# Pooled attention into a four-expert layer: the first tile's loads and order, the first keys' pooling, and the slots of later key and value loads

## The chip, the core and the metric

The kernel runs on one core of a Trainium2 chip. The core has TensorE (matrix products, written to PSUM), VectorE, ScalarE, GpSimd and SyncE, each with its own instruction stream, and 16 DMA engines that all of them share. SyncE and ScalarE issue plain transfers and transposing transfers through the hardware queue; GpSimd issues transfers through the software queue, which can convert f32 to bf16 on the way. The metric is the device time of one execution in microseconds. The profile adds one execution recorded by the hardware profiler.

## The reference

Eight batches, eight heads, 576 tokens of 64 values. Keys and values are averaged over groups of 8 tokens, so each head has 72 pooled keys and values. The attention output, all heads of a token side by side (512 values), feeds four experts, each two matrix products with a ReLU between; the experts' outputs are added with weights from `domain_probs`.

```python
k_p = k.reshape(B, H, Sp, pool, D).mean(axis=3)          # Sp = 72, pool = 8, D = 64
v_p = v.reshape(B, H, Sp, pool, D).mean(axis=3)
scores = scale * np.matmul(q, k_p.transpose(0, 1, 3, 2))
scores = scores - np.max(scores, axis=-1, keepdims=True)
attn = np.exp(scores)
attn = attn / (np.sum(attn, axis=-1, keepdims=True) + 1e-09)
x = np.matmul(attn, v_p)            # (8, 8, 576, 64), then to (4608, 512)
p = domain_probs / (domain_probs.sum(-1, keepdims=True) + 1e-09)
for e in range(4):                  # w1: 512 x 1024, w2: 1024 x 512
    h = np.maximum(x @ w1[e], 0.0)
    out += p[:, e:e + 1] * (h @ w2[e])
```

## The kernel before

**Tiles and groups.** The 4608 tokens are 36 tiles of 128 (`t`); four tiles make a group of 512 (`g`). Attention is computed tile by tile, the expert layer group by group: `up` (L447) makes one block of 128 hidden columns for all 512 tokens of a group (four products of 128x512), `down` (L479) makes the output of one tile from the eight hidden blocks (eight products of 128x512). `collect` (L491) adds a tile's output, weighted, on VectorE and after the fourth expert stores it through SyncE.

**Attention of a tile.** `turn_q` (L301) puts head pairs of the queries on the partitions (for tiles 0 to 8 by TensorE transposes and a ScalarE copy, for later ones by a transposing DMA on SyncE). `scores` (L316) multiplies them with the pooled keys `kT`; its PSUM tile `sc` has a single buffer. `maxima` and `less` (together `less_max`) work on VectorE, `expo` on ScalarE. `attn_T` (L387) turns the exponentials, `context` or `context_rows` (L404) multiplies them with the pooled values `vbd`, a block-diagonal spread made with `mask_v`. In rows form (tile 0 and tiles from 8 on) the division by the row sums is done after the product with the values (`x_sb`, L416); otherwise `normalise` (L377) comes before the turn. For tiles from 8 on `attnT` and `xT` are made by transposing DMAs too.

**Pooling.** `prep_k` (L245) adds the eight rows of a group in three folds on VectorE and places each sum twice, masked, into `kpad`; `prep_kT` (L256) turns it into `kT`, for batches from 2 on by a transposing DMA on SyncE (L259). `prep_v` makes `vbd` likewise. Batch 0 is special: `fold_keys0` folds its keys in three parts as they land, `turn_keys0` transposes them on TensorE, `take_keys0` copies the right halves into the zeroed `kT[0]`; its values are summed by eight products with an identity matrix (`sum_values0`, L611) and spread on VectorE (`spread_values0`, L620).

**Order.** Every engine runs its instructions in the order of the Python code (`manual_schedule`). GpSimd's queue begins with the keys and values of batch 0, then the weights of expert 0 and what follows (L145 to L175). The start (L650 to L716) is written out by hand: tile 0 to tile 3 of group 0 are attended, and expert 0's first products are done tile by tile (`up_tile`, L460). `idle_products(n)` (L568) multiplies a zero tile with itself n times. `split_q(c)` (L564) is ScalarE's conversion of tile c's queries out of `qg`, which one SyncE transfer fills for the four tiles of group 0, token `4p + c` on partition p.

After the start a loop of 36 steps with 12 slots each issues `up` of the next step and `down` of this one, and after each slot what `plan` holds for it. `plan_tile(t, slot)` places a tile's attention, `gate(t)` (a GpSimd copy that waits for the tile's `x_sb`) and `load_q(t + 3)` behind it; `plan_batch(b, slot)` places `prep_k`, `prep_kT` and `prep_v` of a batch at slot + 5, + 8 and + 9, one step before the first tile that needs the batch. The loads of keys and values for batches from 3 on stand in the list `waiting`; for each tile from 8 on, in order, one of them is taken off the list and placed at `base + 6` (L559 to L561), where `base - 2` is the slot in which the tile's plan begins, and so directly behind that tile's gate and query load. `done_batches` counts the batches whose preparation has been planned.

Of the kernel before, what the change touches and what calls it, by code (L numbers as in the profile page):

```python
# [10 lines left out]
ALU = mybir.AluOpType  # L11
AX = mybir.AxisListType
BF16 = mybir.dt.bfloat16
F32 = mybir.dt.float32
# [3 lines left out]
def kernel(  # L18
# [102 lines left out]
    def load_w2(e):  # L121
# [5 lines left out]


    qg = raw.tile([P, H, TPG, D], F32, name="qg")
    nc.sync.dma_start(  # L130
        out=qg[:], in_=q[0][:, 0:G, :].rearrange("h (p c) d -> p h c d", c=TPG)
    )
    dp0 = const.tile([P, TPG, E], F32, name="dp0")
    nc.sync.dma_start(
        out=dp0[:], in_=moe_domain_probs[0:G].rearrange("(p c) e -> p c e", c=TPG)
# [48 lines left out]
    def make_mask_v():  # L184
        nc.vector.tensor_copy(
            out=mask_v[:].rearrange("p a z y d -> p (a z y) d"),
            in_=own[:].rearrange("p a z y -> p (a z y)").unsqueeze(2).to_broadcast(
                [P, NPAIR * 4, D]
            ),
        )  # L190
# [141 lines left out]
    def maxima(t):  # L332
        mxs[t] = soft.tile([P, 2, 4], F32, name="mx")
        nc.vector.reduce_max(out=mxs[t][:], in_=by_head(t), axis=AX.X)  # L334
# [213 lines left out]
    for g in range(2, NG):  # L548
        for i in range(TPG):
            t = g * TPG + i  # L550
            base = (E * g - 5 + i) * SLOTS
            last_b = ((t + 1) * P - 1) // S
            if last_b >= done_batches:
                plan_batch(last_b, base - 2 - SLOTS)
                done_batches += 1
                if last_b + 2 < B:
                    waiting += [(load_k, last_b + 2), (load_v, last_b + 2)]
            plan_tile(t, base - 2, -9 if t > 2 * TPG else 0)
            if waiting:  # L559
                load, b = waiting.pop(0)  # L560
                at(base + 6, load, b)  # L561


    def split_q(c):  # L564
        nc.scalar.copy(out=qrow[c][:], in_=qg[:, :, c, :])


    def idle_products(n):  # L568
        ps = ps_o.tile([P, DM], F32, name="o_ps")
        for _ in range(n):  # L570
            nc.tensor.matmul(ps[:], lhsT=still[:, 0:P], rhs=still[:], start=True, stop=True)  # L571
# [2 lines left out]

    kT[0] = prep.tile([P, NB, P], BF16, name="kT")
    nc.vector.memset(kT[0][:], 0.0)
    kpad0 = prep.tile([P, NB, 2, D], BF16, name="kpad")
    kT_ps = ps_h.tile([P, NB, P], BF16, tag="h", name="kT_ps")

    def fold_keys0(p1, i0, i1):  # L580
        rows = kraw[0][0:p1, i0:i1]
        for n in (4, 2):
            w = n * D
            nc.vector.tensor_add(
                out=rows[:, :, 0:w], in0=rows[:, :, 0:w], in1=rows[:, :, w:2 * w]
            )
        twice = [p1, i1 - i0, 2, D]
        nc.vector.tensor_tensor(
            out=kpad0[0:p1, i0:i1], in0=rows[:, :, 0:D].unsqueeze(2).to_broadcast(twice),
            in1=rows[:, :, D:2 * D].unsqueeze(2).to_broadcast(twice), op=ALU.add,  # L590
        )

    def turn_keys0(p1, i0, i1):
        for i in range(i0, i1):
            nc.tensor.transpose(
                kT_ps[:, i, 0:p1], kpad0[0:p1, i].rearrange("p z d -> p (z d)"),
                ident[0:p1, 0:p1],
            )

    def take_keys0():  # L600
        for z in range(2):
            dst, src = (
                x[z * D:(z + 1) * D].rearrange("x i p -> x (i p)")[:, 0:ROWS].rearrange(
                    "x (a y j) -> x a y j", y=2, j=SP
                )[:, :, z]
                for x in (kT[0], kT_ps)
            )
            nc.vector.tensor_copy(out=dst, in_=src)

# [38 lines left out]
        nc.scalar.copy(out=xT[0][:, :, 0:P], in_=ps[:])  # L648

    idle_products(14)  # L650
    split_q(0)
    split_q(1)
    turn_q(0)
    turn_q(1)
    for part in ((P, 0, 2), (P, 2, 4), (TAIL, 4, 5)):
        fold_keys0(*part)
        turn_keys0(*part)
        idle_products(2)
    take_keys0()
    make_mask_v()  # L660
    scores(0)
    split_q(2)
    turn_q(2)
    less_max(0)
    split_q(3)
    expo(0)
    idle_products(2)
    spread_values0(sum_values0())
    attn_T(0)
    scores(1)  # L670
    maxima(1)
    idle_products(2)
    sums0()
    turn_q(3)
    idle_products(1)
    xT[0] = grp.tile([P, KC, G], BF16, name="xT")
    x0 = context_rows(0)
    idle_products(4)
    turn_x0(x0)
    less(1)  # L680
    expo(1)
    idle_products(2)
    up_tile(0, 0)
    scores(2)
    normalise(1)
    idle_products(4)
    less_max(2)
    domain_probs0()
    for t in range(1, TPG):
        attn_T(t)  # L690
        if t + 1 < TPG:
            expo(t + 1)
        if t == 1:
            idle_products(3)
        else:
            down(0, t - 1, 0, FB // 2)
        context(t)
        if t == 1:
            scores(3)
            up_tile(0, t)  # L700
            down(0, t - 1)
        else:
            down(0, t - 1, FB // 2, FB)
            up_tile(0, t)
        if t + 1 < TPG:
            normalise(t + 1)
        if t == 1:
            less_max(3)
        if t == TPG - 1:
            make_mask_k()  # L710
        collect(0, t - 1)
# [49 lines left out]
```

## Time and profile before

| | us |
|---|---|
| median of 3 runs | 555.86 (554.24 to 556.35) |
| the profiled execution | 556.4 |
| its span, first to last instruction | 554.4 |
| first product of the expert loop (L453) | 36.82 |
| first product of `up_tile` (L469) | 19.01 |
| first key part folded (L584) | 7.79 |
| all of `kT[0]` copied (L608) | 11.76 |
| last 40 products of the chain of waits (L486) begin | 542.05 |

The span is the time between the first and the last instruction of the profiled execution; some 2 us lie around it. A row of the timeline gives start, length, engine, line, operation, and in brackets how long the engine had been idle and what ended that. L numbers are lines of the kernel before. "Landing" of a DMA counts from its issue to the end of its last write. The page's 40 slices show the DMA engines and the granted TensorE clock (in tenths of full speed) over the span:

```profile
PEclk9999999899999999999999999999999999999999
DMA  9999918455745534366535553334333431111002
```

The DMA engines are full for about the first 70 us (the first five slices of 13.9 us), while weights, keys, values and queries arrive; after that they are busy about half the time or less.

### The profile page before, as it was taken

How to read it: one execution, taken by the hardware profiler on the slowest of the kernel's cores; microseconds unless marked ns; L12 is line 12 of the kernel's file. 1: busy time of each engine (PE TensorE's matmuls, PEld its weight loads, DVE VectorE, ACT ScalarE, POOL GpSimd, SP SyncE). 2: the span in 40 equal slices, each digit the busy share in tenths (PEclk: the TensorE clock that was granted, in tenths of full speed). 3: DMA queues.
4: the chain of work that ended last, by engine and by line, in shares of the span. 5: the costliest groups of instructions: out<-in, count | busy, mean ns of one | idle time of the engine just before them, and what ended most of it. 6: DMA issues, size and time to landing. Idle time of an engine off the chain costs nothing.

```text
span 554.4 us, 7323 instructions
## 1 busy us (share of the span) xinstructions
PE 542.0 (98%) x2929; PEld 261.3 (47%) x2929; DVE 264.7 (48%) x456; ACT 213.5 (39%) x355; POOL 70.6 (13%) x120
## 2 busy tenths in 40 slices
PE   7899998999999999999999999999999999999997
PEld 3664553444444444444444444444444444444443
DVE  4874846344644445644463444744474444422223
ACT  3554653233333333333333333333333333333330
POOL 7234002111101100112011100101010000000000
PEclk9999999899999999999999999999999999999999
DMA  9999918455745534366535553334333431111002
GB/s 200 206 200 200 199 8 137 74 80 79 122 82 83 84 59 99 53 84 74 116 48 77 84 116 41 52 41 98 60 54 40 74 74 32 21 39 38 1 0 77
DMA packets 110689, 45.84 MB, mean 83 GB/s; under 512 B 87584, under 2 KB 106016, under 8 KB 110656
## 3 DMA queue, kind: packets, MB, share of 16 engines
q0 software_dynamic: 51472, 22.03, 32.3%
q1 hardware_dynamic: 59184, 23.35, 17.8%
q8 instruction: 23, 0.38, 0.3%
q14 instruction: 10, 0.08, 0.0%
HBM read 45.16 MB, written 9.44 MB: 98 GB/s over the span
## 4 chain that ended last, share of the span: by engine, by line
PE 93%; DMA 3%; DVE 2%; ACT 1%; issue 0%; POOL 0%; SPq 0%; POOLq 0%
PE o_ps L486 44%; PE h_ps L453 43%; PE x_ps L410 2%; PE sc L320 2%; DMA kT<-kpad 1%; PE h_ps L469 1%; DMA kraw<-in_k_dram 1%; PE x_ps L436 1%; PE o_ps L571 0%; DVE acc L501 0%; PE at_ps L394 0%; ACT attnT L395 0%; PE qT_ps L310 0%; DVE kraw L235 0%; DVE vraw L235 0%
## 5 line engine op out<-in xcount | busy, mean ns | idle before, releaser
L457 ACT ACTIVATE h_sb<-h_ps 128x512 bf16<-128x512 f32 x280 | 167.2, 597 | 301.3 <-PE h_ps L453 301.1
L453 PE MATMUL h_ps<-xT,w 128*128 128x512 bf16 x1120 | 275.2, 380 | 0.0
L486 PE MATMUL o_ps<-w,h_sb 128*128 128x512 bf16 x1152 | 272.3, 379 | 0.0
L486 PEld LDWEIGHTS <-h_sb 128*128 128x128 bf16 x1152 | 112.5, 98 | 134.5 <-issue 1.1
L501 DVE SCALAR_TENSOR_TENSOR acc<-o_ps,p_sb,acc 128x512 f32<-128x512 f32 x108 | 81.0, 750 | 180.4 <-PE o_ps L486 180.4
L453 PEld LDWEIGHTS <-w 128*128 128x128 bf16 x1120 | 106.1, 98 | 117.2 <-issue 0.6
L497 DVE TENSOR_SCALAR acc<-o_ps,p_sb 128x512 f32<-128x512 f32 x36 | 27.0, 750 | 62.1 <-PE o_ps L486 62.1
L525 POOL COPY gated<-x_sb 1x1 bf16<-1x1 bf16 x28 | 7.8, 278 | 372.2 <-DVE x_sb L416 372.2
L334 DVE TENSOR_REDUCE mx<-sc 128x8 f32<-128x576 f32 x36 | 27.2, 756 | 14.1 <-PE sc L320 14.1
L108 POOL DMA_DIRECT2D qrow<-in_q_dram x36 | 30.5, 850 | 26.3 <-DMA w<-in_moe_w_dram 15.2
L338 DVE TENSOR_TENSOR d_sb<-sc,mx 128x576 f32<-128x576 f32 x36 | 27.3, 757 | 1.2
L416 DVE SCALAR_TENSOR_TENSOR x_sb<-x_ps,rs 128x512 bf16<-128x512 f32 x29 | 20.1, 692 | 12.5 <-PE x_ps L410 12.1
L351 ACT ACTIVATE attn<-d_sb 128x576 bf16<-128x576 f32 x29 | 19.8, 682 | 3.6 <-DVE d_sb L338 0.5
L372 DVE TENSOR_REDUCE es<-attn 128x8 f32<-128x576 bf16 x28 | 20.8, 744 | 0.0
L320 PE MATMUL sc<-kT,qT 128*128 128x144 bf16 (+1 forms) x160 | 15.3, 229 | 3.1 <-DMA kT<-kpad 2.9
L320 PEld LDWEIGHTS <-qT 128*128 128x128 bf16 (+1 forms) x160 | 11.2, 101 | 11.5 <-issue 5.5
L410 PEld LDWEIGHTS <-attnT 128*128 128x128 bf16 (+1 forms) x160 | 12.2, 100 | 7.3 <-issue 1.3
L410 PE MATMUL x_ps<-vbd,attnT 128*128 128x192 bf16 (+5 forms) x160 | 14.7, 231 | 0.0
L571 PE MATMUL o_ps<-still 128*128 128x512 bf16 x38 | 11.8, 436 | 1.3 <-DVE still L144 1.3
L235 DVE TENSOR_TENSOR vraw<-vraw 128x1280 bf16<-128x1280 bf16 (+1 forms) x14 | 9.2, 654 | 0.2
L235 DVE TENSOR_TENSOR kraw<-kraw 128x1280 bf16<-128x1280 bf16 (+1 forms) x14 | 9.0, 640 | 0.2
L469 PE MATMUL h_ps<-xT,w 128*128 128x128 bf16 x128 | 7.8, 219 | 0.7 <-ACT xT L442 0.4
(76 smaller groups left out, 148.9 us busy)
## 6 DMA issues: line engine op xcount, KB each, us to landing
out_dram<-acc SPq DMA_DIRECT2D x36, 256.0 KB, 2.0
vraw<-in_v_dram POOLq DMA_DIRECT2D x8, 512.0 KB, 7.6
w<-in_moe_w_dram POOLq DMA_DIRECT2D x8, 512.0 KB, 16.1
w<-in_moe_w_dram POOLq DMA_DIRECT2D x4, 1024.0 KB, 16.2
kraw<-in_k_dram POOLq DMA_DIRECT2D x7, 512.0 KB, 7.3
qrow<-in_q_dram POOLq DMA_DIRECT2D x28, 128.0 KB, 3.8
qg<-in_q_dram SPq DMA_DIRECT2D x1, 1024.0 KB, 5.7
kraw<-in_k_dram POOLq DMA_DIRECT2D x2, 256.0 KB, 6.7
```

What stands on the lines that cost most here:

```text
L108: nc.gpsimd.dma_start(out=qrow[t][at:at + n], in_=q[b][:, tok:tok + n, :].rearrange("h p d -> p h d"),)
L320: nc.tensor.matmul(sc[at:at + n, pair // 2, (pair % 2) * PW:(pair % 2 + 1) * PW], lhsT=qT[t][:, pair, at:at + n], rhs=kT[b][:].rearrange(" ...
L334: nc.vector.reduce_max(out=mxs[t][:], in_=by_head(t), axis=AX.X)
L338: nc.vector.tensor_tensor(out=st[t][:], in0=by_head(t), in1=mxs[t][:].unsqueeze(3).to_broadcast([P, 2, 4, SP]), op=ALU.subtract,)
L372: nc.vector.reduce_sum(out=es[:], in_=e, axis=AX.X)
L410: nc.tensor.matmul(ps[at:at + n, h0 * D:(h0 + c1 - c0) * D], lhsT=attnT[t][:, i, at:at + n], rhs=flat[:, c0 * D:c1 * D], start=(i == 0), s ...
L416: nc.vector.scalar_tensor_tensor(out=x_sb[:].rearrange("p (h d) -> p h d", d=D), in0=ps[:].rearrange("p (h d) -> p h d", d=D), scalar=V_ME ...
L453: nc.tensor.matmul(ps[:], lhsT=w1_sb[e][:, kc, fb * P:(fb + 1) * P], rhs=xT[g][:, kc, :], start=(kc == 0), stop=(kc == KC - 1),)
L457: nc.scalar.activation(out=hs[s][:, fb, :], in_=ps[:], func=ACT.Relu)
L486: nc.tensor.matmul(ps[:], lhsT=hs[s][:, fb, i * P:(i + 1) * P], rhs=w2_sb[e][:, fb, :], start=(fb == 0), stop=(fb == FB - 1),)
L497: nc.vector.tensor_scalar_mul(out=accs[t][:], in0=ps[:], scalar1=p_sb[:, e, t:t + 1])
L501: nc.vector.scalar_tensor_tensor(out=accs[t][:], in0=ps[:], scalar=p_sb[:, e, t:t + 1], in1=accs[t][:], op0=ALU.mult, op1=ALU.add,)
```

## The change

Six things change. (1) The first SyncE transfer fetches only tile 0's queries; the other three tiles' queries are fetched by one transfer that ScalarE issues behind `split_q(0)`. (2) The keys of batch 0 are no longer folded on VectorE and transposed: 45 products with the identity add the eight rows and turn them at once into an f32 PSUM tile of the `sc` pool, the two halves of the partitions summing the same eight rows in another order. (3) `make_mask_v` comes first on VectorE. (4) `split_q`, `turn_q` of tiles 1 to 3 move behind `scores(0)`, `maxima(1)`, `context_rows(0)`, `expo(1)` and `scores(2)`; `context_rows(0)` follows `sums0` directly. (5) Fewer idle products stand at other places, 33 where there were 38, and `expo(2)` comes behind `context(1)`. (6) In the planner a waiting load is placed only at a tile t for which the batch of tile t + 1's last token is among those already planned.

```diff
@@ -127,9 +127,8 @@
 
 
     qg = raw.tile([P, H, TPG, D], F32, name="qg")
-    nc.sync.dma_start(
-        out=qg[:], in_=q[0][:, 0:G, :].rearrange("h (p c) d -> p h c d", c=TPG)
-    )
+    q0 = q[0][:, 0:G, :].rearrange("h (p c) d -> p h c d", c=TPG)
+    nc.sync.dma_start(out=qg[:, :, 0, :], in_=q0[:, :, 0, :])
     dp0 = const.tile([P, TPG, E], F32, name="dp0")
     nc.sync.dma_start(
         out=dp0[:], in_=moe_domain_probs[0:G].rearrange("(p c) e -> p c e", c=TPG)
@@ -556,7 +555,8 @@
                 if last_b + 2 < B:
                     waiting += [(load_k, last_b + 2), (load_v, last_b + 2)]
             plan_tile(t, base - 2, -9 if t > 2 * TPG else 0)
-            if waiting:
+
+            if waiting and ((t + 2) * P - 1) // S < done_batches:
                 load, b = waiting.pop(0)
                 at(base + 6, load, b)
 
@@ -574,36 +574,32 @@
 
     kT[0] = prep.tile([P, NB, P], BF16, name="kT")
     nc.vector.memset(kT[0][:], 0.0)
-    kpad0 = prep.tile([P, NB, 2, D], BF16, name="kpad")
-    kT_ps = ps_h.tile([P, NB, P], BF16, tag="h", name="kT_ps")
-
-    def fold_keys0(p1, i0, i1):
-        rows = kraw[0][0:p1, i0:i1]
-        for n in (4, 2):
-            w = n * D
-            nc.vector.tensor_add(
-                out=rows[:, :, 0:w], in0=rows[:, :, 0:w], in1=rows[:, :, w:2 * w]
-            )
-        twice = [p1, i1 - i0, 2, D]
-        nc.vector.tensor_tensor(
-            out=kpad0[0:p1, i0:i1], in0=rows[:, :, 0:D].unsqueeze(2).to_broadcast(twice),
-            in1=rows[:, :, D:2 * D].unsqueeze(2).to_broadcast(twice), op=ALU.add,
-        )
-
-    def turn_keys0(p1, i0, i1):
+    kT_ps = ps_s.tile([P, 2, 512], F32, name="sc")[:].rearrange("p g x -> p (g x)")
+
+
+
+    def sum_keys0(p1, i0, i1):
         for i in range(i0, i1):
-            nc.tensor.transpose(
-                kT_ps[:, i, 0:p1], kpad0[0:p1, i].rearrange("p z d -> p (z d)"),
-                ident[0:p1, 0:p1],
-            )
+            cols = slice(i * P, i * P + p1)
+
+            def add(half, r0, n, **flags):
+                nc.tensor.matmul(
+                    kT_ps[half, cols], lhsT=kraw[0][0:p1, i, r0 * D:(r0 + n) * D],
+                    rhs=ident[0:p1, 0:p1], skip_group_check=True, **flags,
+                )
+
+            for r in range(POOL - 1):
+                add(slice(0, P), r, 2, start=(r == 0 and i in (0, NB - 1)), stop=False)
+            add(slice(0, D), POOL - 1, 1, start=False, stop=True)
+            add(slice(D, P), 0, 1, start=False, stop=True)
 
     def take_keys0():
         for z in range(2):
             dst, src = (
-                x[z * D:(z + 1) * D].rearrange("x i p -> x (i p)")[:, 0:ROWS].rearrange(
-                    "x (a y j) -> x a y j", y=2, j=SP
-                )[:, :, z]
-                for x in (kT[0], kT_ps)
+                x[z * D:(z + 1) * D, 0:ROWS].rearrange("x (a y j) -> x a y j", y=2, j=SP)[
+                    :, :, z
+                ]
+                for x in (kT[0][:].rearrange("x i p -> x (i p)"), kT_ps)
             )
             nc.vector.tensor_copy(out=dst, in_=src)
 
@@ -648,55 +644,56 @@
         nc.scalar.copy(out=xT[0][:, :, 0:P], in_=ps[:])
 
     idle_products(14)
+    make_mask_v()
     split_q(0)
+    nc.scalar.dma_start(out=qg[:, :, 1:TPG, :], in_=q0[:, :, 1:TPG, :])
+    turn_q(0)
+    for part in ((P, 0, 2), (P, 2, 4), (TAIL, 4, 5)):
+        sum_keys0(*part)
+    take_keys0()
+    idle_products(3)
+    scores(0)
     split_q(1)
-    turn_q(0)
     turn_q(1)
-    for part in ((P, 0, 2), (P, 2, 4), (TAIL, 4, 5)):
-        fold_keys0(*part)
-        turn_keys0(*part)
-        idle_products(2)
-    take_keys0()
-    make_mask_v()
-    scores(0)
-    split_q(2)
-    turn_q(2)
     less_max(0)
-    split_q(3)
     expo(0)
     idle_products(2)
     spread_values0(sum_values0())
     attn_T(0)
     scores(1)
     maxima(1)
+    split_q(2)
     idle_products(2)
     sums0()
-    turn_q(3)
-    idle_products(1)
     xT[0] = grp.tile([P, KC, G], BF16, name="xT")
     x0 = context_rows(0)
-    idle_products(4)
+    turn_q(2)
+    idle_products(3)
     turn_x0(x0)
     less(1)
     expo(1)
+    split_q(3)
     idle_products(2)
     up_tile(0, 0)
     scores(2)
+    turn_q(3)
     normalise(1)
-    idle_products(4)
+    idle_products(2)
     less_max(2)
     domain_probs0()
     for t in range(1, TPG):
         attn_T(t)
-        if t + 1 < TPG:
-            expo(t + 1)
         if t == 1:
             idle_products(3)
-        else:
+        elif t + 1 < TPG:
+            expo(t + 1)
+        if t > 1:
             down(0, t - 1, 0, FB // 2)
         context(t)
         if t == 1:
+            expo(2)
             scores(3)
+            idle_products(2)
             up_tile(0, t)
             down(0, t - 1)
         else:
```

## The prediction

> **What bounds the kernel now.** I read the page's engine shares first, then TensorE's waits after the start, the stretches around the one wait found there, the chain of waits through it, and last the timeline and DMA queues of the start.
>
> ```profile
> PE 542.0 (98%) x2929; PEld 261.3 (47%) x2929; DVE 264.7 (48%) x456; ACT 213.5 (39%) x355; POOL 70.6 (13%) x120
> ```
>
> TensorE is busy 542.0 of 554.4 us, so only its 12.4 idle us, stretches at a low clock and the start (where "busy" includes 38 idle products) can be won. After the start (36.8 us) its waits have a single line:
>
> ```profile
> PE sc L320 <- DMA kT<-kpad: 2.9, 1, 2.9
> ```
>
> That is tile 9's scores waiting for the transposed keys of batch 2. The timeline's GpSimd rows, the chain, and the stretches around it (columns: stretch, length, busy us of PE, PEld, DVE, ACT, POOL, granted clock, DMA share, GB/s):
>
> ```profile
> 89.07 0.88 POOL L108 DMA_DIRECT2D qrow<-in_q_dram  x1
> 89.94 0.76 POOL L80 DMA_DIRECT2D kraw<-in_k_dram  x1
> ...
> 89.62 7.65 DMA kT<-kpad
> 97.27 0.14 issue
> 97.41 0.64 PE sc L320 x4
> 98.04 1.71 PE h_ps L453 x4
> 99.75 2.15 PE o_ps L486 x8
> ...
> 94.50:97.40 2.90, 0.03 (x1) 0.02 (x1) 0.00 (x0) 0.60 (x1) 0.00 (x0) 0.94 1.06 210
> 97.40:100.50 3.10, 3.09 (x11) 1.42 (x12) 1.51 (x2) 0.71 (x2) 0.00 (x0) 0.51 0.45 123
> ```
>
> The key transpose is issued at 89.62 and lands after 7.65 us; a key load (batch 3) goes out 0.32 us after it. After the wait TensorE runs for 3 us at clock 0.51.
>
> In the start, the timeline's rows that set the first expert product:
>
> ```profile
> 12.72 1.25 PE L614 MATMUL v_ps<-vraw,ident 128*128 128x320 bf16 x8
> 14.01 1.29 DVE L623 TENSOR_TENSOR vbd<-v_ps,mask_v 128x512 bf16<-128x512 f32 x2
> 15.59 0.76 DVE L334 TENSOR_REDUCE mx<-sc 128x8 f32<-128x576 f32 x1 [0.28 <-PE sc L320]
> 16.40 0.17 DVE L640 TENSOR_SCALAR es<-es_ps 128x8 f32<-128x8 f32 x1
> 17.19 0.69 DVE L416 SCALAR_TENSOR_TENSOR x_sb<-x_ps,rs 128x512 bf16<-128x512 f32 x1 [0.39 <-PE x_ps L410]
> 19.01 1.95 PE L469 MATMUL h_ps<-xT,w 128*128 128x128 bf16 x32 [0.24 <-ACT xT L648]
> ```
>
> The chain of waits names the keys (issued 1.32, second part landed 9.05, kT done 11.77). But the values bind almost as soon: they are issued at 3.39 and 4.15 and take 8.8 and 8.2 us, so they land at 12.19 and 12.35, and v_ps, vbd, the second maxima and x_sb follow each other from there. This decides what the start can win.
>
> **Part 1: key loads moved away from key transposes (L559).** By the new condition load_k(3) leaves slot 42 (the slot of prep_kT(2)) for slot 54. The queue shifts by one place: key and value loads of batches 3 to 5 go into slots 54, 66, 78, 102, 114, 126; those of batches 6 and 7 stay. Only slot 126 is new, and it has no key transpose.
>
> What it removes: scores(9) could have started at 93.50 + 0.86 = 94.36 (the four products before it, at the chain's price for four) and started at 97.41: 3.05 us. Then 0.64 + 1.71 + 2.15 = 4.50 us of products stand where the chain at 80 us has 0.25 + 0.86 + 1.73 = 2.84: 1.66 us of low clock. Together 4.7 us.
>
> Is the wait gone then? The other five key transposes have no key load beside them, but the same query load just before and stores behind; they land after 4.3, 4.1, 3.7, 4.0 and 4.5 us, and none is waited for. Here 94.36 - 89.62 = 4.74 us are free. So 0 us of wait is left, at worst 7.65 - 4.74 = 2.9 again if the key load was not the cause. I take 4.7.
>
> What moves: each load issues two DMAs on GpSimd's queue behind gate(t) and load_q; the next in that queue is the gate a tile (14 us) later, so nothing waits. Key loads land after 7.3 us (median): k3 issued near 108.8 lands near 116, and prep_k(3) precedes the transpose at 151.8. v5, the one at the new slot, goes out near 195 for the transpose at 282.1. That cover is tens of us.
>
> The Trainium skill ("TensorE: Matmul & The Clock Gate", HAM oscillation) gives the rule that TensorE should have no idle gap over some 3.4 us. By that alone a 2.9 us gap would cost only itself and this part would be 3.05 us, the whole 4.0 instead of 5.6. The row above (0.51 after a gap of 2.9) speaks against it, and I go by the row.
>
> **Part 2: the start.** *The loads.* The queries' first transfer shrinks from 1024 to 256 KB, in 256-byte pieces. Bounds: a query load of the main loop reads as much in such pieces and lands after 2.4 us at best; the whole qg took 5.7. So it lands between 3.2 and 6.5; I take 4.2, near the small load. ScalarE casts it (0.61), issues the other 768 KB at about 4.9, and goes on with qT(0), which TensorE's 14 idle products (to 6.23) hold back anyway.
>
> The queue rows for 5.0 to 6.5 us show how the two kinds of transfer stand beside each other (packets, MB, share):
>
> ```profile
> q0 software_dynamic: 147, 0.15, 61.5%
> q1 hardware_dynamic: 392, 0.27, 58.4%
> ```
>
> Half each. Before 5.0 the software queue moves nothing; full speed is about 400 GB/s read. The rest of the queries then needs 0.79 MB / 0.2 = 3.9 us, after 1.1 us from issue to first packet (qg: 0.81 to 1.9) and with 1.0 us from last data to landing (qg: 5.5 to 6.5): 4.9 + 6.0 = 10.9.
>
> *The values (V).* q, k and v are the same 3.4 MB as before through a path that is full from 3.5 us on, so V moves only by what the start of the stream loses. At 177 and 274 GB/s in the third and fourth microsecond 0.35 MB had moved by 3.7 us; now it is the first 0.26 MB, so 0.09 / 0.4 = 0.25 us later: V = 12.6. Lower bound 11.9 (the rest of the queries gets a smaller share); upper bound 13.65 (the software queue starts at 5.0 as before, and 3.7 to 5.0 is empty).
>
> The skill's "DMA: Bandwidth & Descriptors", Specifications, wants at least 512 bytes a piece for full speed, which speaks against the 256-byte pieces. An estimate by it counts them double: 0.26 / 0.4 = 0.65 us instead of 0.25, the whole 5.2 instead of 5.6.
>
> *The keys.* Removed: six folds and three additions on VectorE (2.83 us), five transposes. Added: 45 products at (1.95 - 0.22) / 31 = 0.056 us, 2.5 us in a TensorE that waits there, of which 9 x 0.056 + 0.17 = 0.7 follow the last landing. The two copies read f32 now: 0.62 as before, to 0.76 by the maxima's rate (576 in 0.76). Keys near 8.3 give kT near 9.7 (was 11.77), d_sb at 9.7 + 0.45 + 0.80 + 0.78 = 11.7. ScalarE must first do split_q(1) (from 10.9, 0.62) and qT(1) (0.4 + 0.59), so attn is ready at 13.3. But transposing it stands behind v_ps, free at 12.7 + 1.1 = 13.8: the two microseconds gained on the keys are worth nothing. The mask (0.69), taken from VectorE's chain, is likewise hidden behind the values.
>
> *The sum of the start.* v_ps 12.7 to 13.95 (was 12.72 to 13.97), spread 1.29, maxima 0.76, es to x_sb 0.42 (as es, rs are spaced now), with 0.1 of handovers: x_sb starts at 16.5, was 17.19. Its two other feeders are in time: es_ps by 15.3 (attn^T from 13.8: 0.44, 0.69, 0.28), x_ps by 15.8, now right behind, where before turn_q(3) and an idle product held it to 17.16. That is 0.69. Behind it, the transposes of tile 1's attention waited to 21.91 behind four idle products, with attn ready at 21.57; now two and turn_q(3) (0.23) end at 21.71: 0.2. split_q(3) ahead of the ReLU hides in the products; expo(2) behind the xT copy makes tile 2's attention about 0.7 later (25.77 to 26.5) for transposes at 27.92. Start: 0.9 us.
>
> Do weights hold it? w1 of expert 0, second half: issued 6.72 + 10.7 = 17.4, needed at 19.0; w2: 7.46 + 16.2 = 23.7, needed at 25.3. Covered by about 1.5 us; beyond that the start would wait for them.
>
> Bounds of the start: V = 11.9 gives 1.6 gained. V = 13.65 gives 0.15 lost, and the rest of the queries at 13 instead of 11 (2 more on a path where each microsecond past 11 counts) some 1.5 lost.
>
> **Sum.** 4.7 + 0.9 = 5.6 of the profiled span of 554.4: 548.8. The profiled execution took 556.4 (2.0 around the span), 0.5 above the median 555.86; taken from the median: 550.3.
>
> **Rivals.**
> 1. *A new wait in the start* (part 1 as forecast): the software queue is cold until 5 us, or the rest of the queries is late; TensorE's gap before the values (11.1 to 12.7) may also cost clock. For it: no software packet before 5.0. Against: main-loop key loads need nothing like 3.7 us to begin. Start 0.3 to 2.5 longer: 551.5 to 553.7, centre 552.3.
> 2. *The change doesn't do what it says*: the query load and stores still delay the key transpose. For it: the query load at 89.07 precedes it. Against: the five others. Only the start counts: 555.0.
> 3. *Slower*: the rest of the queries queues behind the weights. Weight loads take 16.1 us to land (median) in that stretch: 4.9 + 16.1 = 21, and split_q(1), turn_q(1), and behind it in TensorE's order v_ps, are 10 late: 555.86 - 5.6 + 10 = 560.3. It decides from a landing at 11 + 5.6 + 2.8 = 19.4. Against: the half shares, and a key transpose beside a key load lost 3.5 us, not 16.
>
> **Chances.** A difference of 0.5% (2.8 us) is about what can be told. Forecast 0.62 (own range 549.5 to 551.5); rival 1 0.20, of it 0.17 below 553.1; rival 2 0.10; rival 3 0.05; a better start than bounded 0.03. Faster 0.82, same 0.13, slower 0.05. The range 548.8 to 553.2 leaves out rivals 2 and 3 and the ends.
>
> **What would show it.** No wait on kT, clock 1.00 around 90 to 100 us, key transposes landing in 3.7 to 4.5. Values landing at 12 to 13, x_sb starting at 16.5, first up product at 18.3, expert loop (36.82) at 35.9. kT ready two microseconds earlier with attn waiting for TensorE. It is wrong if scores(9) waits on, if turn_q(1) waits past 11.7, or a load at a new slot is waited for.

## The result, and the profile after

The changed kernel takes 558.95 us (median of 6 runs, 558.71 to 559.22) where the kernel before took 555.1 in the same session. The ratio is 1.0068, with a 95% interval of 1.005 to 1.0085: slower by 0.7%. The profiled execution took 559.0 with a span of 557.0; before it was 556.4 and 554.4. Of 65 executions of the kernel before in the later sessions, 43 had a mean granted clock of 0.998 or more and took 554.0 us (median), and 22 had 0.997 or less and took 555.8; the profiled one (0.997) is of the second kind, so the difference of the spans, +2.6, and that of the medians, +3.85, do not measure quite the same.

TensorE's waits of the changed kernel (engine, tile, line, releaser: us in total, times, longest):

```profile
PE qT_ps L309 <- ACT qrow L565: 5.9, 1, 5.9
PE o_ps L571 <- DVE still L143: 1.3, 1, 1.3
PE sc L319 <- DVE kT L604: 0.4, 1, 0.4
```

The wait for `kT` of batch 2 that led the list before is gone. In its place TensorE waits 5.9 us, once, for the second tile's queries. The same wait in the timeline of TensorE (start, length, line, operation, idle time before it and its releaser):

```profile
6.95 0.39 PE L309 MATMUL qT_ps<-ident,qrow 128*128 128x128 bf16 x4
7.17 3.20 PE L586 MATMUL sc<-ident,kraw 128*128 128x128 bf16 x45
...
11.49 0.41 PE L319 MATMUL sc<-kT,qT 128*128 128x144 bf16 x4 [0.36 <-DVE kT L604]
17.79 0.61 PE L309 MATMUL qT_ps<-ident,qrow 128*128 128x128 bf16 x4 [5.89 <-ACT qrow L565]
18.19 1.06 PE L571 MATMUL o_ps<-still 128*128 128x512 bf16 x2
19.05 2.34 PE L610 MATMUL v_ps<-vraw,ident 128*128 128x320 bf16 x8
...
25.90 1.28 PE L468 MATMUL h_ps<-xT,w 128*128 128x128 bf16 x20 [0.24 <-ACT xT L644]
```

`turn_q(1)` (17.79) stands ahead of the values' product in TensorE's order, so `v_ps` starts at 19.05 where it started at 12.72, and takes 2.34 us where it took 1.25. The first `up_tile` product comes at 25.90 (19.01 before), the first product of the expert loop at 43.50 (36.82 before). The chain of waits over the first 26 us says what was late:

```profile
3.94 0.01 ACT qrow L565
3.95 13.14 DMA qg<-in_q_dram
17.09 0.02 issue
17.12 0.63 ACT qrow L565
17.74 0.05 issue
17.79 0.61 PE qT_ps L309 x4
```

The rest of the queries, issued by ScalarE at 3.95, landed 13.14 us later. Two rows by queue for 10.0 to 17.2 us (packets, MB, share of the 16 engines) show it (q10) beside the weights, values and keys of the software queue (q0):

```profile
q0 software_dynamic: 1059, 1.04, 85.1%
q10 hardware_dynamic: 809, 0.61, 33.6%
```

The stretches around the wait, and the one of tiles 8 and 9 (stretch, length, busy us and count of PE, PEld, DVE, ACT, POOL, granted clock, DMA share, GB/s):

```profile
17.40:20.40 3.00, 2.61 (x12) 1.49 (x13) 0.00 (x0) 1.50 (x3) 1.22 (x2) 0.50 1.24 207
...
93.50:100.00 6.50, 6.45 (x35) 3.11 (x34) 4.50 (x9) 2.39 (x4) 1.53 (x2) 1.00 0.80 138
```

The clock is 0.50 from 13.49 to 23.73 in the clock's records, that is in the later part of the wait and for 5.9 us behind it. It is 1.00 around 94 to 100, where it had been 0.51 from 97.4 to 100.5. The transposed keys of batch 2 are now issued at 96.30, with no key load beside them (DMA issues of 95.7 to 97.2, us to landing):

```profile
kT<-kpad SPq DMA_TRANSPOSE x1, 4.2
```

The account closes with three terms. The start grew by 43.50 - 36.82 = 6.68. From the loop's first product to the start of the last accumulation on VectorE it took 513.90 us before (550.72 - 36.82) and 509.37 after (552.87 - 43.50): 4.53 less, which is the first part of the change. The end behind that grew by 0.45. Together 6.68 - 4.53 + 0.45 = +2.60, the difference of the spans.

### The profile page after: what moved, and what is told of

It is laid out like the page before. It is cut to its first block, busy times and chain, and to the rows that moved or that the text cites. A ratio compares the mean times of both kernels' runs of the same rounds, so it can differ in the third digit from the quotient of the medians.

```text
span 557.0 us, 7332 instructions
## 1 busy us (share of the span) xinstructions
PE 541.7 (97%) x2907; PEld 264.6 (48%) x2964; DVE 262.2 (47%) x447; ACT 213.4 (38%) x355; POOL 71.0 (13%) x120
## 3 DMA queue, kind: packets, MB, share of 16 engines
q1 hardware_dynamic: 59184, 22.57, 17.2%
## 4 chain that ended last, share of the span: by engine, by line
PE 95%; DMA 3%; issue 1%; ACT 1%; DVE 0%
PE o_ps L485 44%; PE h_ps L452 43%; DMA qg<-in_q_dram 3%; PE x_ps L409 2%; PE sc L319 2%; PE h_ps L468 1%; PE x_ps L435 1%; PE o_ps L571 1%; PE qT_ps L309 0%; PE at_ps L393 0%; PE v_ps L610 0%; ACT attnT L394 0%; DVE acc L500 0%; ACT qrow L565 0%; ACT xT L644 0%
## 5 line engine op out<-in xcount | busy, mean ns | idle before, releaser
L452 PE MATMUL h_ps<-xT,w 128*128 128x512 bf16 x1088 | 271.8, 379 | 1.5
L415 DVE SCALAR_TENSOR_TENSOR x_sb<-x_ps,rs 128x512 bf16<-128x512 f32 x29 | 20.1, 692 | 12.3 <-PE x_ps L409 11.9
L319 PEld LDWEIGHTS <-qT 128*128 128x128 bf16 (+1 forms) x160 | 11.3, 101 | 8.7 <-issue 2.5
L571 PE MATMUL o_ps<-still 128*128 128x512 bf16 x30 | 11.7, 519 | 1.5 <-DVE still L143 1.3
L309 PE MATMUL qT_ps<-ident,qrow 128*128 128x128 bf16 x36 | 3.7, 229 | 5.9 <-ACT qrow L565 5.9
## 6 DMA issues: line engine op xcount, KB each, us to landing
qg<-in_q_dram ACTq DMA_DIRECT2D x1, 768.0 KB, 13.1
```

The costliest lines, as they stand in the source:

```text
L319: nc.tensor.matmul(sc[at:at + n, pair // 2, (pair % 2) * PW:(pair % 2 + 1) * PW], lhsT=qT[t][:, pair, at:at + n], rhs=kT[b][:].rearrange(" ...
L415: nc.vector.scalar_tensor_tensor(out=x_sb[:].rearrange("p (h d) -> p h d", d=D), in0=ps[:].rearrange("p (h d) -> p h d", d=D), scalar=V_ME ...
L452: nc.tensor.matmul(ps[:], lhsT=w1_sb[e][:, kc, fb * P:(fb + 1) * P], rhs=xT[g][:, kc, :], start=(kc == 0), stop=(kc == KC - 1),)
```

## The experiments

All experiments are stand-ins. In each of them the transposing transfers of SyncE (`kT` of later batches, `qT`, `attnT` and `xT` of later tiles) are replaced by plain transfers of the same bytes, so these tiles are copied and not turned. Stand-ins are compared with each other, and the ratios are to the kernel before as it is, in the same session. The first four ran in one session and the others in three more; the median of the kernel before was 554.07 to 555.15, with its mix of clocks. The start, where the queries of the first four tiles, the first keys and the first values are handled by TensorE, is that of the real kernels.

The last column is from the profiled execution of each, which for t_tile1_first (560.91), t_folded_keys (553.38) and t_best (554.21) was the longest of its runs.

| stand-in | median us | ratio [95%] | loop's first product |
|---|---|---|---|
| t_before | 551.99 | 0.9949 [0.993, 0.9967] | 36.81 |
| t_after | 558.76 | 1.0065 [1.0043, 1.0088] | 43.03 |
| t_whole_queries | 551.63 | 0.9936 [0.9914, 0.9959] | 36.62 |
| t_planner_only | 551.90 | 0.9936 [0.9917, 0.9956] | 36.83 |
| t_tile1_first | 559.53 | 1.0085 [1.0059, 1.011] | 45.44 |
| t_rest_on_sync | 552.39 | 0.9962 [0.9946, 0.9978] | 37.13 |
| t_gap_filled | 557.95 | 1.0055 [1.0033, 1.0077] | 42.44 |
| t_folded_keys | 552.99 | 0.9961 [0.9947, 0.9975] | 38.35 |
| t_folded_warm | 552.67 | 0.9959 [0.9946, 0.9973] | 37.76 |
| t_later_turn | 556.86 | 1.0045 [1.0031, 1.0059] | 41.76 |
| t_best | 553.35 | 0.9983 [0.9971, 0.9994] | 39.09 |
| t_scalar_early | 552.32 | 0.9963 [0.995, 0.9975] | 36.84 |

### Stand-ins of both kernels: t_before and t_after

```diff
-            nc.sync.dma_start_transpose(
-                out=kT[b][:], in_=pads[b][:].rearrange("p i z d -> p (i z d)")
+            nc.sync.dma_start(
+                out=kT[b][:], in_=pads[b].rearrange("p i z d -> p i (z d)")
```

and the like for `qT`, `attnT` and `xT`; `kpad` gets a third, unused part so that the plain copy has its shape. Expected of the stand-in of before:

> Stand-in of the kernel before: every turning DMA of SyncE (kT, qT, attnT, xT of later tiles) is a plain DMA of the same bytes from on-chip memory to on-chip memory, so these four tiles are copied and not turned; all else is the same. The start doesn't use them: expert loop starting at 36.8 as before. Whether scores(9) waits for kT is open: Theory A (the key load issued beside it delays any small transfer of SyncE) expects a wait of 1 to 3 us at scores(9); Theory E (only the turning is slow beside a load) expects none, and a total about 4.5 us under before.

Expected of the stand-in of after:

> The same stand-in of the changed kernel. Theory A: second query transfer landing near 17, turn_q(1) waiting 5 to 6 us, loop starting at 43 to 44, no wait at scores(9). Against the stand-in of before: later by 6.7 less what scores(9) waited there.

The stand-in of after shows the same 5.9 us wait, with the loop's first product at 43.03. The stand-in of before has no wait at all at tile 9's scores: with the same loads in the same slots they start at 94.36 and the clock stays at 1.00. The DMA issues between 89.0 and 90.5 us (size, us to landing), the kernel before first:

```profile
kraw<-in_k_dram POOLq DMA_DIRECT2D x1, 512.0 KB, 8.9
qrow<-in_q_dram POOLq DMA_DIRECT2D x1, 128.0 KB, 4.4
...
kT<-kpad SPq DMA_TRANSPOSE x1, 7.7
```

and its stand-in:

```profile
kraw<-in_k_dram POOLq DMA_DIRECT2D x1, 512.0 KB, 9.0
kT<-kpad SPq DMA_DIRECT2D x1, 160.0 KB, 3.0
```

Beside the same key load the turning transfer took 7.7 us to land and the plain one 3.0. So the delay belonged to the turning transfer beside a key load. The stand-ins therefore hold nothing of part 1's gain, and their differences measure the start alone. No run has part 1 by itself with the turning transfers. The changed kernel shows it together with the new start; there the six key transposes land after 4.0 to 4.8 us. That the later start alone would have removed the wait is not excluded by a run, but the transpose moved by just the 6.68 us of the loop (89.62 to 96.30), so the key load beside it would have moved along.

### The queries loaded whole: t_whole_queries

The changed kernel, but with the queries of all four tiles in one SyncE transfer again.

```diff
-    nc.sync.dma_start(out=qg[:, :, 0, :], in_=q0[:, :, 0, :])
+    nc.sync.dma_start(out=qg[:], in_=q0)
...
-    nc.scalar.dma_start(out=qg[:, :, 1:TPG, :], in_=q0[:, :, 1:TPG, :])
```

> The stand-in of the changed kernel with one part undone: the first SyncE transfer fetches all four tiles' queries again, and ScalarE issues no transfer. Theory A (the second query transfer is the whole loss of the start): no wait at turn_q(1), values landing near 12.4, x_sb starting at 16.3 to 16.6, expert loop starting at 35.5 to 36.0. Rival B (the 45 key products or the new hand-written order cost the start): the loop still starts after 38.

This one edit takes the loop's first product from 43.03 to 36.62, 6.41 us, and the wait is gone. Everything else that the change does to the start is worth 36.81 - 36.62 = 0.2 us against t_before, not 0.9. TensorE's timeline shows why:

```profile
12.36 0.41 PE L319 MATMUL sc<-kT,qT 128*128 128x144 bf16 x4 [0.36 <-DVE kT L604]
12.60 0.39 PE L309 MATMUL qT_ps<-ident,qrow 128*128 128x128 bf16 x4
12.82 0.59 PE L571 MATMUL o_ps<-still 128*128 128x512 bf16 x2
13.26 1.25 PE L610 MATMUL v_ps<-vraw,ident 128*128 128x320 bf16 x8
```

The values' product is held by the keys: 45 products from 8.02 to 11.24, the copies from 11.28 to 12.20, then the scores, `turn_q(1)` and two idle products. In t_before `kT` is complete at 11.75. `x_sb` starts at 17.19, as before the change.

### The planner's condition alone: t_planner_only

```diff
-            if waiting:
+            if waiting and ((t + 2) * P - 1) // S < done_batches:
```

> The stand-in of before with the planner's new condition alone. Theory A: loop starting at 36.8, no wait at scores(9), and under the stand-in of before by what that wait and the low clock after it were there (4.5 us if the wait is 3 us, nothing if there is none). Rival C (the moved loads meet other transfers): a new wait elsewhere in the loop.

551.90 us against t_before's 551.99: no difference, as there is no wait to remove in the stand-in. It shows the other half of part 1: TensorE waits for no load in a new slot.

### Bytes or pieces: t_tile1_first

ScalarE issues tile 1's queries alone, a third of the bytes in as many pieces (1024 of 256 bytes), then tiles 2 and 3 (1024 of 512).

```diff
-    nc.scalar.dma_start(out=qg[:, :, 1:TPG, :], in_=q0[:, :, 1:TPG, :])
+    nc.scalar.dma_start(out=qg[:, :, 1:2, :], in_=q0[:, :, 1:2, :])
+    nc.scalar.dma_start(out=qg[:, :, 2:TPG, :], in_=q0[:, :, 2:TPG, :])
```

> The stand-in of the changed kernel; ScalarE issues the rest of the queries as two transfers, tile 1 alone (256 KB in 1024 pieces of 256 bytes) and then tiles 2 and 3 (512 KB in 1024 pieces of 512 bytes). Theory A1 (beside the busy software queue the pieces of the two queues go one for one, so a transfer takes its count of pieces, not its bytes): tile 1 lands near 16 to 17, as the 768 KB did, and tiles 2 and 3 near 24 to 25; loop starting at 43 or later. Rival A2 (the queues share by bytes or by time): tile 1 lands at 10.5 to 12 and turn_q(1) waits under 1 us.

The DMA issues of 3.5 to 5.0 us, with their landing, and the queues from 10.0 to 17.2 us:

```profile
qg<-in_q_dram ACTq DMA_DIRECT2D x1, 512.0 KB, 19.4
qg<-in_q_dram ACTq DMA_DIRECT2D x1, 256.0 KB, 12.6
```

```profile
q0 software_dynamic: 1112, 1.09, 89.0%
q10 hardware_dynamic: 1149, 0.36, 31.8%
```

256 KB took 12.6 us to land, where 768 KB in as many pieces took 13.3 (t_after; 13.1 in the changed kernel). In these 7.2 us the two queues moved 1112 and 1149 packets, nearly one for one, though one kind carries three times the bytes of the other (1.09 MB to 0.36). The time goes by pieces, not by bytes. The loop starts still later (45.44), since tiles 2 and 3 now land 19.4 us after their issue and are waited for as well; the other three executions were some 1.4 us shorter than the profiled one.

### Issued earlier, by SyncE or by ScalarE: t_rest_on_sync, t_scalar_early

The same transfer of 768 KB, issued by SyncE right behind tile 0's (1.31 us), or by ScalarE ahead of all its work (0.81 us).

```diff
     nc.sync.dma_start(out=qg[:, :, 0, :], in_=q0[:, :, 0, :])
+    nc.sync.dma_start(out=qg[:, :, 1:TPG, :], in_=q0[:, :, 1:TPG, :])
...
-    nc.scalar.dma_start(out=qg[:, :, 1:TPG, :], in_=q0[:, :, 1:TPG, :])
```

(t_scalar_early has `nc.scalar` in the added line.)

> The stand-in of the changed kernel; the rest of the queries is issued by SyncE right behind the first transfer, before the software queue has work, instead of by ScalarE at 3.95. Theory A: both land before 8, no wait at turn_q(1), loop starting within 0.5 of the whole-queries run (36.6). Rival F (splitting the load into 256 and 768 byte pieces is what costs): landing after 10, loop above 38.

> The changed kernel with the rest of the queries still issued by ScalarE, but ahead of everything, at about 0.8 to 1.3 us, instead of behind the cast of the first tile at 4.0. Theory A (what made it late is the time at which it met the values' pieces, not the engine that issued it): most of it moves before the values' first piece, it lands at 8.5 to 10.5, no wait at the second tile's queries, the keys land 1 to 2 us later as in t_rest_on_sync, expert loop at 36.6 to 37.6, ratio 0.995 to 0.997. Rival F (a transfer issued by ScalarE takes 3.5 us to its first piece and is slow on its own): first piece at 4.3 or later, landing at 12.5 to 14, a wait of 1 to 2 us, loop 38 to 39.5, ratio 0.998 to 1.001.

Both remove the wait: loops at 37.13 and 36.84. The landings, t_rest_on_sync (issues up to 5.0 us):

```profile
qg<-in_q_dram SPq DMA_DIRECT2D x1, 768.0 KB, 7.9
...
qg<-in_q_dram SPq DMA_DIRECT2D x1, 256.0 KB, 3.2
```

and t_scalar_early (issues up to 2.0 us):

```profile
qg<-in_q_dram ACTq DMA_DIRECT2D x1, 768.0 KB, 6.5
qg<-in_q_dram SPq DMA_DIRECT2D x1, 256.0 KB, 4.8
kraw<-in_k_dram POOLq DMA_DIRECT2D x1, 256.0 KB, 6.9
```

From the same engine, in the same 1024 pieces, the transfer takes 6.5 us instead of 13.3 (t_after) when it is issued 3.2 us earlier. So the issuing engine is not the cause (rival F falls). Most of the transfer moves before the software queue's first piece (5.45): by the packet records it moved about 205 pieces in each half microsecond from 4.5 to 5.5, beside some 50 small ones of SyncE's queue, against 65 in the changed kernel. It lands at 7.3, earlier than the 8.5 to 10.5 expected. The price appears elsewhere: tile 0's queries land after 4.8 us instead of 3.2 (t_scalar_early), and the key products wait 1.5 us for their keys (2.3 in t_rest_on_sync). That is why neither beats t_whole_queries.

The Trainium skill ("DMA: Bandwidth & Descriptors", Issuing engines are not separate DMA queues) states that transfers started by different engines run on the same 16 DMA engines and interleave. These runs agree, and show in what measure here: about one piece of each queue for one of the other (1112 to 1149 packets in t_tile1_first; 733 to 734 from 10.0 to 15.5 us in the changed kernel).

### The same wait, kept warm: t_gap_filled

```diff
     scores(0)
+    idle_products(28)
     split_q(1)
```

> The stand-in of the changed kernel with 28 idle products (28 x 0.216 = 6.0 us) between scores(0) and turn_q(1), where TensorE waits. It tells the price of the low clock from that of the wait. Theory A: the landing stays at 17, the clock stays 1.00, and the loop starts 1 to 2 us earlier than in the stand-in of the changed kernel (43.0): 41 to 42. If the clock costs nothing: 43.0 to 43.4.

The clock stays at 1.00 and the loop starts at 42.44, 0.59 us before t_after's 43.03. But in this execution the queries landed later, 14.0 us after their issue where it was 13.3, so the second tile's transposes started 0.70 us later (t_gap_filled and then t_after):

```profile
18.69 0.40 PE L309 MATMUL qT_ps<-ident,qrow 128*128 128x128 bf16 x4 [0.68 <-ACT qrow L565]
```

```profile
17.99 0.61 PE L309 MATMUL qT_ps<-ident,qrow 128*128 128x128 bf16 x4 [5.91 <-ACT qrow L565]
```

From there to the loop it is 23.75 us against 25.04. TensorE's stretch behind the wait, t_gap_filled and then t_after:

```profile
17.00:20.40 3.40, 2.72 (x19) 1.46 (x18) 0.00 (x0) 1.79 (x3) 0.74 (x1) 1.00 1.25 206
```

```profile
17.00:20.40 3.40, 2.41 (x11) 1.40 (x12) 0.00 (x0) 1.78 (x3) 1.40 (x2) 0.50 1.24 207
```

So the low clock is worth some 1.3 us of the 6.41, within the 1 to 2 expected; the medians, with whatever landings they had, differ by 0.81. Of t_after's 6.8 us at half clock (13.84 to 20.67) 4.2 fell into the wait itself. In the changed kernel, with 5.9 us of it behind the wait, the same count gives an estimate of 25.71 - 23.75 = 2.0 us.

### The order alone: t_later_turn

The late landing stays, but `split_q(1)` and `turn_q(1)` move behind the turning of tile 0's attention.

```diff
     scores(0)
-    split_q(1)
-    turn_q(1)
     less_max(0)
...
     attn_T(0)
+    split_q(1)
+    turn_q(1)
     scores(1)
```

> The changed kernel with the second tile's queries split and turned behind the turning of the first tile's attention instead of right behind the first scores. Theory A (the transfer lands at 17 whatever waits for it; only what stands behind the waiting transposes pays): the transposes of the second tile still start at 17.5 to 18.2, but the values' product is back at 13 to 14, the wait shrinks to about 3 us, and the expert loop's first product comes at 39.3 to 40.2 (43.03 in t_after): about 555.4 us, ratio 1.000. Rival (the late queries hold the whole start by whatever way): 42 or later, ratio 1.005.

```profile
13.95 1.26 PE L610 MATMUL v_ps<-vraw,ident 128*128 128x320 bf16 x8 [1.65 <-DMA vraw<-in_v_dram]
15.05 0.44 PE L393 MATMUL at_ps<-ident,attn 128*128 128x128 bf16 x5
18.48 0.40 PE L309 MATMUL qT_ps<-ident,qrow 128*128 128x128 bf16 x4 [2.99 <-ACT qrow L565]
19.55 0.66 PE L319 MATMUL sc<-kT,qT 128*128 128x144 bf16 x4 [0.68 <-ACT qT L313]
...
24.16 1.95 PE L468 MATMUL h_ps<-xT,w 128*128 128x128 bf16 x32 [0.24 <-ACT xT L644]
```

The values' product is free again (13.95, now held by the values) and the wait is halved to 2.99. But the loop starts at 41.76, 1.3 us earlier than t_after and not the 3 or so that theory A said: behind the late transposes TensorE waits 0.68 us more for the copy of `qT`, runs 3.4 us at half clock, and the whole rest of the start still stands behind it. By the medians the new order takes back 1.9 of the 7.1 us between t_after and t_whole_queries. One of its nine runs, at a mean clock of 0.999, took 555.61, near theory A's 555.4; the others (0.992 to 0.997) took 556.57 to 557.83. So a part of what theory A missed goes with the clock, and even then the transfer's landing, not the place of its reader, is the larger part.

### The keys by folds: t_folded_keys, t_folded_warm

t_whole_queries with the first keys folded on VectorE and transposed, as before the change; the second with two idle products behind each part again.

```diff
     for part in ((P, 0, 2), (P, 2, 4), (TAIL, 4, 5)):
-        sum_keys0(*part)
+        fold_keys0(*part)
+        turn_keys0(*part)
+        idle_products(2)
```

(The last line stands in the second alone.)

> The whole-queries run with the first keys folded on VectorE and transposed as before (nine VectorE instructions, five transposes) instead of summed by 45 products. Theory G (the products are slower than the folds: 0.071 us each, and the copies of f32 take 0.92 instead of 0.62): kT ready 0.4 us earlier than the 12.2 there, v_ps 0.4 to 0.6 earlier than 13.26, loop starting at 36.0 to 36.3 instead of 36.6. Rival (the products are free or gain, hidden behind the values): loop at 36.6 or later.

> As t_folded_keys, with two idle products put back behind each part of the keys. Theory G (the 45 products are slower than the folds, and t_folded_keys lost only to the clock): clock 1.00 throughout, keys turned and copied 0.2 to 0.5 us before t_whole_queries' 12.20, expert loop's first product at 36.1 to 36.5 (36.62 there), about 551.3 us, ratio 0.993. Rival (the fold was never late: the values and the rest of the start decide): first product at 36.5 to 36.8, ratio as t_whole_queries. If the clock still falls: 37 or later.

The copies of `kT` end at 11.82 in t_folded_warm, 0.4 us before t_whole_queries' 12.20: the folds are faster, as theory G has it. But in both profiles the clock fell, and the loop starts at 38.35 and 37.76. The stretches of t_folded_warm, and one of t_before:

```profile
7.50:11.00 3.50, 1.55 (x11) 0.53 (x9) 2.65 (x9) 1.10 (x2) 3.43 (x5) 0.99 1.23 202
11.00:14.30 3.30, 3.30 (x15) 1.82 (x16) 0.98 (x3) 0.00 (x0) 1.58 (x4) 0.50 1.23 203
```

```profile
7.50:11.00 3.50, 1.98 (x15) 0.77 (x13) 2.65 (x9) 1.72 (x4) 3.12 (x4) 1.00 1.20 193
```

With TensorE busy 1.55 of 3.5 us the next 3.4 us ran at half clock; with 1.98 of 3.5 they did not. So the folds' advantage was not seen in these profiles. Two of the ten runs of t_folded_warm had a mean clock of 0.999 or 1.0 and took 551.22 and 551.45; the five of t_whole_queries, in another session, took 551.15 to 551.69. If the folds win at full clock, it is by no more than a few tenths, and that stays open. The 45 products are slower, and keep TensorE busy.

### A version meant to beat both: t_best

The planner's condition; tiles 1 to 3 of the queries on GpSimd's queue, converted on the way; folds with idle products; `turn_q(1)` and `turn_q(2)` one step later.

```diff
+    def load_q0(c):
+        nc.gpsimd.dma_start(out=qrow[c][:], in_=q0[:, :, c, :])
...
-    turn_q(1)
     less_max(0)
...
     attn_T(0)
+    turn_q(1)
     scores(1)
```

> A version meant to beat both: the planner's new condition, the first tile alone by SyncE, the three other tiles by GpSimd's queue straight to bf16 behind the values and behind the first weights, the keys folded on VectorE with idle products behind each part, the second and third tiles turned one step later. If the queue of the weights takes these transfers in its order without holding up the first weights by more than they hold: expert loop's first product at 34.8 to 35.8, 550 us, ratio 0.990. Rival (the second tile's queries or the first weights come too late in that queue): 36.8 or later, ratio 0.994 or more.

The first weights and queries came in time and `v_ps` started at 12.12, 1.1 us earlier than in t_whole_queries. It was lost again:

```profile
14.15 0.45 PE L400 MATMUL at_ps<-ident,attn 128*128 128x128 bf16 x5 [0.76 <-ACT attn L357]
14.44 0.39 PE L316 MATMUL qT_ps<-ident,qrow 128*128 128x128 bf16 x4
15.87 0.43 PE L326 MATMUL sc<-kT,qT 128*128 128x144 bf16 x4 [1.05 <-ACT qT L320]
```

`turn_q(1)` so close to `scores(1)` costs the copy of `qT` in the open (1.05, and 0.94 for tile 2), and the clock is 0.50 from 16.33 to 19.75. Ratio 0.9983, and 553.35 us against t_before's 551.99: slower. The clock explains only some of it, since runs at a mean clock of 0.998 to 1.0 still took 553.0 to 553.5. Of the stand-ins none beats t_whole_queries.

## Why the prediction was wrong

The forecast was 550.3 us, and the kernel took 558.95. Both parts were predicted by their own sums; one held and one failed. The table goes by the spans of the two profiled executions:

| term | predicted | measured |
|---|---|---|
| part 1: wait at `scores(9)` and its low clock | -4.7 | -4.53 |
| part 2: the start | -0.9 | +6.68 |
| the end | 0 | +0.45 |

**Part 1 was right** in mechanism, and in size for the profiled execution: no wait on `kT`, clock 1.00 from 93.5 to 107, no wait for a load in a new slot. That the key load was the cause is supported more strongly than by the prediction's comparison with five other transposes: the plain transfer in the same place landed after 3.0 us, the turning one after 7.7. But the prediction took the whole 4.7, 1.66 of it low clock, off a median, and only a third of the executions of the kernel before show a lower clock. By medians part 1 is worth about 3.0: (555.15 - 551.99) for the kernel before against its stand-in, less (558.95 - 558.76) for the changed one. The start takes 558.76 - 551.99 = 6.8 by the same count, an estimate as far as the stand-ins differ from the kernels in nothing else. Why some executions keep the clock was not profiled.

**The step that failed** is the landing of the rest of the queries, 10.9 by the prediction and 17.1 in the trace: "Half each. [...] The rest of the queries then needs 0.79 MB / 0.2 = 3.9 us, after 1.1 us from issue to first packet". Two things in it were wrong.

*Half shares.* The row that it rests on (5.0 to 6.5 us: 61.5% and 58.4%) is an average over a hand-over, and busy shares are not bytes (0.15 MB and 0.27 in that row). Counting the packet records of the two traces by half microseconds (software queue, then hardware queue) shows it:

```
before   5.0: 7, 212     5.5: 66, 143    6.0: 74, 37     6.5: 102, 10
after    9.5: 56, 56    10.0: 64, 63    10.5: 65, 65    11.0: 67, 68
```

In before one queue was ending while the other began, and the two halves never stood beside each other. In after the queues share piece for piece. A piece of the software queue is 1024 bytes as written, one of the rest of the queries is 768, and at 65 pieces in 0.5 us that is 0.10 MB/us, not 0.2: about 8 us for the 1024 pieces in place of 3.9.

*The first packet.* It came at 7.6, 3.7 us after the issue, not 1.1: the 1.1 was read from a transfer issued into empty queues. In t_scalar_early, with only SyncE's load of tile 0 ahead of it, it came after 1.8 us. Why it took 3.7 is not shown.

So 3.95 (4.9 predicted: the issue did not wait for the end of the cast) + 3.7 + 9.1 (to the last packet at 16.7) + 0.35 = 17.1. The rest followed from TensorE's order as the prediction's own test said ("if turn_q(1) waits past 11.7").

**Rival 3 had the path**: the rest of the queries late, and behind it in TensorE's order the second tile's transposes and the values' product. It did not have the way, since the transfer went piece for piece beside the software queue and not behind it. It had the landing at 21 by the weights' 16.1 us, and so a larger loss (560.3); that this lies near the 558.95 measured is in part luck. Its argument against was the same half shares. Its point of decision, a landing at 19.4, was too late as well: it still counted 0.9 us won in the start, 4.7 in part 1 and no low clock, and 17.1 was enough.

**The miss adds up.** The start was 7.58 us longer than forecast (6.68 + 0.9). Of this, 6.41 is the split load's late landing (t_after against t_whole_queries, some 1.3 of it low clock by t_gap_filled), 0.7 is gain that the rest of part 2 did not bring (0.2 of 0.9), and 0.47 is that the changed kernel's own start came later than its stand-in's (43.50 against 43.03), with 10.2 us at half clock where the stand-in had 6.8.

**Smaller steps.** The small query load landed at 3.92 (4.2 predicted). The values landed at 12.8 and 13.3 (12.6, inside the bounds of 11.9 to 13.65). The key products were mis-sized: 3.20 us for 45, 0.071 each and not 0.056; they began only at 7.17, behind idle products that ran to 7.1 and not 6.23; and the copies from f32 took 0.92, not 0.62 to 0.76. So `kT` was ready at 11.3, not 9.7. With that the sentence that the keys are hidden behind the values was wrong: in t_whole_queries `kT` (12.20) is later than the fold's (11.75) and holds `v_ps` at 13.26, which took the 0.69 us of the forecast. The 0.2 us at tile 1's attention held.

The loss was thus not a trade-off within part 1 or of the new products: an estimate from these runs for the change with the queries loaded whole is 558.95 - (558.76 - 551.63) = 551.8 us, which no run here shows with the turning transfers.

## What to carry to other kernels

Splitting a load to get its first part sooner can put its rest beside whatever other queues start in between: issue the rest before them, or leave the load whole. When two queues run at once, count pieces and not bytes, and take the rate from a stretch in which both are in full flow. And ask of every late landing what stands behind its reader in the reader's own queue: here one set of four transposes held the values and the whole start. Before a gain read from one profiled execution is taken off a median, look whether the other executions show the same clock.

## What the runs showed of the hardware

- Two DMA queues, a hardware queue and the busy software queue, moved one piece for one, whatever the pieces' sizes: 256 KB in 1024 pieces took 12.6 us and 768 KB in 1024 pieces 13.3; the latter took 6.5 when it met that queue only at its end.
- The turning transfer of the keys landed after 7.7 us beside a 512 KB key load, a plain one of the same bytes after 3.0; without a key load beside it the turning one took 3.7 to 4.8.
- TensorE's clock halved without a long gap: t_folded_warm had no wait over 1.4 us, and 1.55 us of work in 3.5, before 3.4 us at 0.50. The Trainium skill ("TensorE: Matmul & The Clock Gate", HAM oscillation) asks for no idle gap over some 3.4 us; these rows and the 2.9 us gap before the change speak for the busy share of such a stretch as the thing to watch.
- In the clock's records the clock changes in steps of 3.41 us (stretches of 3.4, 6.8 and 10.2 us at 0.50). Laid over the spans of all fourteen profiles, every such step at full clock in which TensorE was busy for 0.43 or less was followed by a lower clock; no step with 0.55 or more was; of the four from 0.45 to 0.49 two were. A gap of under 3 us therefore counts by where it falls in these steps, which may be why executions of one kernel differ; that is argued, not shown.
- Half the clock for 6.8 us cost some 1.3 us of time, because 4.2 of it passed in the wait.
